# PSUM clears, column copies and delta moved out of a VectorE chain at the seam between a weight stage and the last pass

## The chip, the cores and the metric

The kernel runs on one core of one Trainium2 chip. The metric is the device time in microseconds (us), as the median of several executions. On one core there is no second die to compare, so a run counts as fast when it is within 1.5% of the fastest run of the same kernel, and only fast runs are compared.

## The reference

The reference is the forward and the backward pass of two identical layers. Each has an attention of one new token over a cached K and V, and an MLP. The output and nine gradients are wanted, among them those of both caches. All arrays are bf16.

```python
# B=2, Sq=1, D=1024; Hq=32, Hkv=4, Sk=16384, Dh=128; F=3584
def attn(x, k_cache, v_cache, wq, wo):
    q = (x @ wq) as [B, Hq, 1, Dh]
    p = softmax(q k^T * Dh**-0.5)          # each kv head serves 8 q heads
    return (p v) as [B, 1, Hq*Dh] @ wo
def mlp(x, w1, b1, w2, b2):
    return gelu(layernorm(x) @ w1 + b1) @ w2 + b2
x = x + attn(layernorm(x), ...); x = x + mlp(x, ...)     # layer 1
x = x + attn(layernorm(x), ...); x = x + mlp(x, ...)     # layer 2, same weights and caches
# outputs: x, and the vjp of (x, K, V, wq, wo, w1, b1, w2, b2) with grad_out
```

For the backward pass of attention, "do" is the gradient of o (what comes back through wo, unnormalised here, then scaled), "delta" is the sum over the head dimension of do times o, and "ds" is p times (do v - delta). The gradients of K and V need ds and p for both layers, so they are made in one last pass over the caches.

## The kernel before

The program is ordered by hand. Everything that lies in SBUF comes from pools opened once, and a pool begins where the one ahead of it ends. The seven rotating load tiles ("ld") take every chunk of the caches and of the weights that is not kept in SBUF, 1 MB or 0.9 MB each. Ahead of them lie the pools of constants and vectors. The cuts of code leave lines out ("..."), and most comments in them are added for the reader.

```python
LDW = 4096
NLD = 7
const = ctx.enter_context(tc.tile_pool(name="const", bufs=1))
vec = ctx.enter_context(tc.tile_pool(name="vec", bufs=1))
pers = ctx.enter_context(tc.tile_pool(name="pers", bufs=1))
ld = ctx.enter_context(tc.tile_pool(name="ld", bufs=NLD))       # [128, 4096] bf16: 8192 bytes a partition
res = ctx.enter_context(tc.tile_pool(name="res", bufs=1))       # kept chunks of K and V
ktp = ctx.enter_context(tc.tile_pool(name="ktp", bufs=4))
...
e_all = pers.tile([128, G, NP, 2, 8, 2], BF16, name="e_all")
hot3 = const.tile([128, 128], BF16, name="hot3")
...
        t = held_tiles[keep] if keep else ld.tile([128, LDW], BF16, name="kv_" + w, tag="ld")
```

The seam that the change is about is the end of the wo stage of layer 1 and the start of the last pass. A row of wo is either turned by TensorE and multiplied there, or dotted by VectorE:

```python
            self.dotted = range(4, self.J, 5)          # of wo's 32 rows: 4, 9, 14, 19, 24, 29
...
    for j in range(4, wob.J):
        ...
        wob.products(j, dops, gA_all[:, :, lsl(0)])    # TensorE, for rows that are not dotted
    only["e"] = None
    TP = [pt([128, 8, 128], BF16, "tpm%d" % i) for i in range(2)]
    for t in TP:
        V.memset(t[:].bitcast(F32), 0.0)               # two PSUM tiles cleared by VectorE
    do_delta(0, pairs(dops, HQ), wob)                  # dof, doT_bf, dprod, sum, split of delta
    ...
    cols = {}                                          # the columns that TensorE transposes
    for w in "VK":
        cols[w] = vec.tile([128, G, 2, 8], BF16, name="cols" + w)
        for k in range(2):
            src = saved["a%d" % k]["qT_bf" if w == "K" else "doT_bf"]
            V.tensor_copy(out=cols[w][:, :, k, :], in_=src[:])
    ...
    qs = [make_qm(w, order[0]) for w in "VK"]          # transposes of the columns
    for c in range(NCH):
        ...                                            # scores, + delta, ds
```

Copies out of PSUM are shared between ScalarE and VectorE by a running estimate of each engine's load (`load`), unless `only["e"]` names one engine.

## Time and profile before

| | before |
|---|---|
| time, median of three runs | 1166.01 us (1165.72 to 1171.62) |
| span of the profiled run | 1165.4 us |
| read from and written to HBM | 348.14 MB, 98.58 MB |
| TensorE, VectorE, ScalarE busy | 82%, 55%, 48% |

The prediction shows the rows of the page for clock and transfers, the stretches from 720 us on, and the timeline of the seam. What it does not show is how the long loading stages ahead of the seam run. These are three of their stretches before the change, in the view of busy time by stretches (columns as the prediction explains them):

```profile
20.00:100.00 80.00, 64.23 (x1335) 55.70 (x1336) 34.45 (x72) 32.25 (x128) 0.00 (x0) 0.94 1.01 419
100.00:200.00 100.00, 81.07 (x1521) 64.84 (x1520) 39.32 (x92) 38.67 (x187) 0.00 (x0) 0.77 1.02 414
300.00:400.00 100.00, 86.92 (x1720) 71.30 (x1717) 47.49 (x105) 44.82 (x199) 0.00 (x0) 0.90 1.01 418
```

The last three columns are clock, DMA share and GB/s. The DMA engines are busy all the time (1.01, 1.02) while TensorE has room (64.23 of 80 us). So the bytes that the DMA engines move per microsecond set the pace of these stages, and the number to keep in mind is 414 to 419 GB/s at a full share. The page's groups agree: TensorE's largest waits here are for load tiles (the last two columns are the idle time just before the group and what ended most of it).

```profile
L418 PE MATMUL tp<-ident,kv_V 128*128 128x128 bf16 x864 | 70.3, 227 | 10.0 <-DMA kv_V<-in_A_v_cache_dram 8.2
...
L450 PE MATMUL acc_all<-kv_V,e_all 128*16 128x256 bf16 x864 | 45.8, 292 | 28.7 <-DMA kv_V<-in_A_v_cache_dram 16.9
```

### The profile page before, as it was taken

The page shows a single profiled execution, that of the slowest core. Times are in us where ns is not written, and L with a number is a line of the kernel's source. Part 1 is how long each engine was busy: PE and PEld are TensorE (multiplying, and loading weights), DVE is VectorE, ACT ScalarE, POOL GpSimd, SP SyncE. Part 2 cuts the span into 40 slices and gives each one's busy share as a digit, 9 for nine tenths or more (in the row PEclk, how much of TensorE's full clock was granted, in tenths as well). Part 3 has the DMA queues.
Part 4 walks back from the last instruction along what each step waited for, and adds up shares of the span by engine and source line. Part 5 has one row for each costly group of instructions (what it writes and reads, how often), then busy time and mean ns, then how long its engine had stood idle before and what let it go on. Part 6 is the DMA issues. An engine that isn't in the chain of part 4 may idle for free. (4 is left out here: it accounts for less than half of the span.)

```text
span 1165.4 us, 39945 instructions
## 1 busy us (share of the span) xinstructions
PE 955.5 (82%) x17565; PEld 733.2 (63%) x17565; DVE 639.5 (55%) x1344; ACT 562.3 (48%) x1410; POOL 63.9 (5%) x113
## 2 busy tenths in 40 slices
PE   4888895497879875889987799788998988998786
PEld 3866773487767765888776688565555554555452
DVE  1545451133545433454845355867777877787674
ACT  0544351022535430344554444467677866686673
POOL 0000000000000000000000000001111111111111
PEclk9988785587988875999998889797777877797795
DMA  9999999998999989999999999687999999999996
GB/s 370 418 419 418 419 419 397 395 360 352 418 419 414 418 306 418 388 357 408 365 414 412 338 353 350 251 325 299 374 402 422 419 419 418 420 421 418 422 419 247
DMA packets 89130, 449.30 MB, mean 386 GB/s; under 512 B 7026, under 2 KB 7026, under 8 KB 49788
## 3 DMA queue, kind: packets, MB, share of 16 engines
q1 hardware_dynamic: 72204, 348.17, 74.9%
q0 software_dynamic: 16752, 98.59, 20.6%
q8 instruction: 137, 2.24, 0.8%
q14 instruction: 37, 0.30, 0.1%
HBM read 348.14 MB, written 98.58 MB: 383 GB/s over the span
## 5 line engine op out<-in xcount | busy, mean ns | idle before, releaser
L152 ACT COPY kT<-tp 128x512 int32<-128x512 int32 x209 | 122.8, 587 | 257.5 <-PE tp L418 246.5
L155 DVE COPY kT<-tp 128x1024 bf16<-128x1024 bf16 x159 | 108.6, 691 | 112.2 <-PE tp L418 99.2
L418 PE MATMUL tp<-ident,kv_K 128*128 128x128 bf16 x1728 | 147.1, 235 | 3.5 <-DMA kv_K<-in_A_k_cache_dram 3.5
L418 PEld LDWEIGHTS <-kv_K 128*128 128x128 bf16 x1728 | 111.6, 105 | 4.1 <-DMA kv_K<-in_A_k_cache_dram 4.1
L163 DVE CAST big<-xm 128x512 bf16<-128x512 f32 (+1 forms) x138 | 89.8, 685 | 31.3 <-PE xm L1222 14.4
L160 ACT CAST big<-xm 128x512 bf16<-128x512 f32 (+1 forms) x159 | 86.7, 594 | 27.8 <-PE xm L1081 16.8
L571 PEld LDWEIGHTS <-kT 128*128 128x128 bf16 x2048 | 76.7, 98 | 28.0 <-issue 22.1
L571 PE MATMUL sc<-qT_bf,kT 128*128 128x8 bf16 x2048 | 92.1, 171 | 0.7 <-issue 0.7
L268 PE MATMUL wtp<-ident,wt 128*128 128x128 bf16 x928 | 77.1, 231 | 3.7 <-issue 2.4
L418 PE MATMUL tp<-ident,kv_V 128*128 128x128 bf16 x864 | 70.3, 227 | 10.0 <-DMA kv_V<-in_A_v_cache_dram 8.2
L304 PEld LDWEIGHTS <-wt 128*128 128x128 bf16 x1696 | 49.0, 103 | 46.0 <-issue 14.7
L535 ACT ACTIVATE e_all<-sc,negm 128x64 bf16<-128x64 f32 x256 | 77.2, 345 | 1.2 <-DVE negm L530 1.2
L163 DVE CAST keepK<-xm 128x512 bf16<-128x512 f32 x94 | 61.1, 685 | 16.1 <-PE xm L1222 12.4
L450 PE MATMUL acc_all<-kv_V,e_all 128*16 128x256 bf16 x864 | 45.8, 292 | 28.7 <-DMA kv_V<-in_A_v_cache_dram 16.9
L155 DVE COPY wT<-wtp 128x1024 bf16<-128x1024 bf16 (+1 forms) x65 | 41.5, 645 | 48.7 <-PE wtp L268 45.2
L152 ACT COPY wT<-wtp 128x512 int32<-128x512 int32 (+1 forms) x59 | 33.5, 568 | 69.2 <-PE wtp L268 60.5
L160 ACT CAST keepK<-xm 128x512 bf16<-128x512 f32 x103 | 55.4, 592 | 22.4 <-PE xm L1222 21.3
L160 ACT CAST keepV<-xm 128x512 bf16<-128x512 f32 (+1 forms) x91 | 49.4, 594 | 34.9 <-PE xm L1222 28.8
L418 PEld LDWEIGHTS <-kv_V 128*128 128x128 bf16 x864 | 55.5, 102 | 11.8 <-DMA kv_V<-in_A_v_cache_dram 8.9
L163 DVE CAST keepV<-xm 128x512 bf16<-128x512 f32 (+1 forms) x81 | 52.8, 685 | 18.1 <-PE xm L1222 14.1
L268 PEld LDWEIGHTS <-wt 128*128 128x128 bf16 x928 | 58.9, 103 | 4.4 <-issue 2.9
L535 ACT ACTIVATION_READ_ACCUMULATOR e_all<-sc,negm 128x1 f32 x256 | 60.2, 235 | 0.0
(344 smaller groups left out, 1774.2 us busy)
## 6 DMA issues: line engine op xcount, KB each, us to landing
kv_K<-in_A_k_cache_dram SPq DMA_DIRECT2D x81, 1024.0 KB, 12.3
kv_V<-in_A_v_cache_dram SPq DMA_DIRECT2D x81, 1024.0 KB, 12.1
out_dram<-big POOLq DMA_DIRECT2D x36, 1024.0 KB, 17.7
wt<-in_A_wo_dram SPq DMA_DIRECT2D x32, 1024.0 KB, 10.3
wt<-in_B_w_dram SPq DMA_DIRECT2D x32, 896.0 KB, 14.3
out_dram<-keepK POOLq DMA_DIRECT2D x22, 1024.0 KB, 17.3
out_dram<-keepV POOLq DMA_DIRECT2D x18, 1024.0 KB, 16.2
wt<-in_A_wq_dram SPq DMA_DIRECT2D x16, 1024.0 KB, 9.1
```

The costliest lines, as they stand in the source:

```text
L152: S.copy(out=dst.bitcast(I32), in_=src.bitcast(I32))
L155: V.tensor_copy(out=dst, in_=src)
L160: S.copy(out=dst, in_=src)
L163: V.tensor_copy(out=dst, in_=src)
L268: PE.transpose(tp[:, o, :], wv[:, j, (o0 + o) * 128:(o0 + o + 1) * 128], ident[:])
L304: PE.matmul(fps[:, jo, :].rearrange("p (a b) -> p a b", b=2), lhsT=wv[:, j, jo * 128:(jo + 1) * 128], rhs=xT_bf[:, j0 + j, :].unsqueeze(1) ...
L418: PE.transpose(tp[:, j, :], cv[:, b * 8 + j, :], ident[:])
L450: PE.matmul(self.acc[cg:cg + 16, :], lhsT=coef(u), rhs=self.cv[:, t:t + 2, :].rearrange("p t d -> p (t d)"), start=False, stop=True, tile_ ...
L535: S.activation(out=e_all[:, g, f * half:(f + 1) * half, l, h, :], in_=sc[g][f][:, h, :].rearrange("p (a b) -> p a b", b=2), func=ACT.Exp, ...
L571: PE.matmul(sc[g][f][:, :, t % TH], lhsT=kT[:, j, :], rhs=q_bf[:, g, :], start=True, stop=True)
```

## The change

The change is meant to shorten the VectorE chain of the seam. Row 29 of wo is turned rather than dotted. The two clears go to ScalarE, as copies of a zero constant. The columns are written straight from dof, and the other column copies go ahead of an earlier stage. Delta is split after the transposes have been issued. The balance of copies is reset at each switch.

```diff
     e_all = pers.tile([128, G, NP, 2, 8, 2], BF16, name="e_all")
+    zero1 = const.tile([128, 1], F32, name="zero1")
+    V.memset(zero1[:], 0.0)
...
+    def copies_on(e):
+        only["e"] = e
+        load["A"] = load["D"] = 0.0
...
-            self.dotted = range(4, self.J, 5)
+            self.dotted = range(4, FJ, 5)              # FJ = 28: row 29 of wo is turned
...
-        doT_bf = vec.tile([128, G, 8], BF16, name=f"doT_bf{l}")
-        V.tensor_copy(out=doT_bf[:], in_=dof[:])       # (layer 1's tile goes; cols["V"] takes its place)
...
+    cols = {}                                          # now ahead of the w1 pass
...
-    only["e"] = None
+    copies_on(None)
     TP = [pt([128, 8, 128], BF16, "tpm%d" % i) for i in range(2)]
     for t in TP:
-        V.memset(t[:].bitcast(F32), 0.0)
-    do_delta(0, pairs(dops, HQ), wob)
+        S.copy(out=t[:].bitcast(F32), in_=zero1[:].to_broadcast([128, 512]))
+    dof = do_scaled(0, pairs(dops, HQ), wob,
+                    lambda b, dof: do_store(0, dof[:, b * HKV:(b + 1) * HKV], cols["V"][:, b * HKV:(b + 1) * HKV, 0, :]))
+    dl_bank = delta_mm(0, dof)
...
     qs = [make_qm(w, order[0]) for w in "VK"]
+    delta(0, dl_bank)
     for c in range(NCH):
```

More of the change, by code (lines that the diff above doesn't have):

```diff
@@ L830, in attn_out_bwd, with do_scaled @@
         _, dops = w_pass(A_wo, HD, D, "do_ps", gT_bf=gA_all[:, :, lsl(l)])
-        return do_delta(l, dops)
-    def do_delta(l, dops, ahead=None):
+        doT_bf = saved[f"a{l}"]["doT_bf"] = vec.tile([128, G, 8], BF16, name=f"doT_bf{l}")
+        dof = do_scaled(l, dops)
+        do_store(l, dof[:], doT_bf[:])
+        delta(l, delta_mm(l, dof))
+        return doT_bf
+    def do_scaled(l, dops, ahead=None, half=lambda b, dof: None):
         sv = saved[f"a{l}"]
         dof = wrk.tile([128, G, 8], F32, name="dof")
-        for b in range(2):
+        for b in (1, 0):
             V.tensor_tensor(out=dof[:, b * HKV:(b + 1) * HKV, :].rearrange("p k r -> p (k r)"), in0=dops[:, :, b],
@@ L840, in do_delta, with do_store, delta_mm, delta @@
                 r_ = sv["rbc"][:, b * HKV:(b + 1) * HKV, :].rearrange("p k r -> p (k r)")
-                V.tensor_tensor(out=dof[:, b * HKV:(b + 1) * HKV, :].rearrange("p k r -> p (k r)")[:, 4:HQ:5],
-                                in0=ahead.dp[:, :, b], in1=r_[:, 4:HQ:5], op=ALU.mult)
-        doT_bf = vec.tile([128, G, 8], BF16, name=f"doT_bf{l}")
-        V.tensor_copy(out=doT_bf[:], in_=dof[:])
+                V.tensor_tensor(out=dof[:, b * HKV:(b + 1) * HKV, :].rearrange("p k r -> p (k r)")[:, 4:FJ:5],
+                                in0=ahead.dp[:, :, b], in1=r_[:, 4:FJ:5], op=ALU.mult)
+            half(b, dof)
+        return dof
+    def do_store(l, dof, dst):
+        V.tensor_copy(out=dst, in_=dof)
+    def delta_mm(l, dof, bank=None):
+        sv = saved[f"a{l}"]
         prod = wrk.tile([128, G, 8], F32, name="dprod")
         V.tensor_tensor(out=prod[:], in0=dof[:], in1=sv["oT"][:], op=ALU.mult)
-        dlp = part_sum(prod[:].rearrange("p g r -> p (g r)"), G * 8, "dl_ps")
+        bank = pm_([128, 512], F32, "dl_ps") if bank is None else bank
+        PE.matmul(bank[:, 0:G * 8], lhsT=onesf[:], rhs=prod[:].rearrange("p g r -> p (g r)"), start=True, stop=True)
+        return bank
+    def delta(l, bank):
+        dlp = bank[:, 0:G * 8]
         rest_ = wrk.tile([128, G * 8], F32, name="dl_rest")
-        V.tensor_scalar(out=rest_[:], in0=dlp[:], scalar1=-1.0, scalar2=None, op0=ALU.mult)
+        V.tensor_scalar(out=rest_[:], in0=dlp, scalar1=-1.0, scalar2=None, op0=ALU.mult)
         part = wrk.tile([128, G * 8], BF16, name="dl_part")
@@ L861, in do_delta @@
                 V.tensor_tensor(out=rest_[:], in0=rest_[:], in1=part[:], op=ALU.subtract)
-        saved[f"a{l}"]["doT_bf"] = doT_bf
-        return doT_bf
     wq_v = A_wq.rearrange("(j p) n -> p j n", p=128)
@@ L938 @@
     mlp_slope(0)
-    only["e"] = "A"
+    copies_on("A")
     g2 = attn_in_bwd(1, g3, dn1, lambda: some(rest, 2), lambda: some(rest, 3))
@@ L955 @@
         w2b.products(j, dhps, gM_all[:, :, lsl(0)])
-    only["e"] = None
+    copies_on(None)
     mlp_hidden_bwd(0, pairs(dhps, FJ), w2b)
     x4 = mlp_out(1, fps[:, 0:DJ * WIDE].rearrange("p (j b) -> p j b", b=WIDE)[:, :, 0:2])
+    cols = {}
+    for w in "VK":
+        cols[w] = vec.tile([128, G, 2, 8], BF16, name="cols" + w)
+        for k in range(2):
+            if w + str(k) != "V0":
+                V.tensor_copy(out=cols[w][:, :, k, :], in_=saved["a%d" % k]["qT_bf" if w == "K" else "doT_bf"][:])
+    dq0 = vec.tile([128, G, 8], F32, name="dqT0")
+    dn0 = vec.tile([128, DJ, 2], F32, name="dn0")
+    V.memset(dn0[:], 0.0)
     sv = saved["m0"]
@@ L967 @@
     V.tensor_copy(out=dm[:], in_=dmps[:])
-    only["e"] = "A"
+    copies_on("A")
     dn = ln_bwd(dm[:], sv["y2"][:], sv["rstd2"][:], "dn", lambda: some(rest, 2), lambda: some(rest, 3))
@@ L991 @@
         wob.products(j, dops, gA_all[:, :, lsl(0)])
-    only["e"] = None
+    copies_on(None)
     TP = [pt([128, 8, 128], BF16, "tpm%d" % i) for i in range(2)]
     for t in TP:
-        V.memset(t[:].bitcast(F32), 0.0)
-    do_delta(0, pairs(dops, HQ), wob)
+        S.copy(out=t[:].bitcast(F32), in_=zero1[:].to_broadcast([128, 512]))
+    dof = do_scaled(0, pairs(dops, HQ), wob,
+                    lambda b, dof: do_store(0, dof[:, b * HKV:(b + 1) * HKV], cols["V"][:, b * HKV:(b + 1) * HKV, 0, :]))
+    dl_bank = delta_mm(0, dof)
     rowsA = ld.tile([128, LDW], BF16, name="rowsA", tag="ld")
@@ L1153 @@
     qms = {}
-    cols = {}
-    for w in "VK":
-        cols[w] = vec.tile([128, G, 2, 8], BF16, name="cols" + w)
-        for k in range(2):
-            src = saved["a%d" % k]["qT_bf" if w == "K" else "doT_bf"]
-            V.tensor_copy(out=cols[w][:, :, k, :], in_=src[:])
     def make_qm(w, g):
@@ L1229, in kv_pair @@
             store(dst[g, :, c * TC:(c + 1) * TC, :], stgs[w, i][:].rearrange("p (t d) -> p t d", d=128), stgs[w, i])
-    dq0 = vec.tile([128, G, 8], F32, name="dqT0")
-    dn0 = vec.tile([128, DJ, 2], F32, name="dn0")
-    V.memset(dn0[:], 0.0)
     dwq_v = out_4.rearrange("(j p) n -> p j n", p=128)
```

## The prediction

> **What bounds the kernel now.** I read the page first. It has one core, so there is no die to compare; the span is 1165.4 us.
>
> ```profile
> PEclk9988785587988875999998889797777877797795
> DMA  9999999998999989999999999687999999999996
> GB/s 370 418 419 418 419 419 397 395 360 352 418 419 414 418 306 418 388 357 408 365 414 412 338 353 350 251 325 299 374 402 422 419 419 418 420 421 418 422 419 247
> ```
>
> Each column is 29.1 us. The transfers are at 9 or more of ten in nearly every slice; the last pass (gradients of the caches and weights, stores beside loads) runs at 418 to 422 GB/s. The only hole is in slices 25 to 27, about 728 to 815 us: DMA digits 6, 8, 7 and 251 to 325 GB/s. The change touches exactly that hole, so I cut it into stages with the view of busy time by stretches (columns: length; busy us of TensorE, weight loads, VectorE, ScalarE, GpSimd with instruction counts; granted clock; DMA share; GB/s).
>
> ```profile
> 720.00:741.00 21.00, 19.81 (x441) 18.68 (x441) 16.54 (x41) 16.12 (x28) 0.00 (x0) 1.00 0.93 339
> 741.00:748.00 7.00, 1.20 (x9) 0.81 (x10) 5.66 (x29) 0.00 (x0) 0.00 (x0) 0.58 0.84 349
> 748.00:764.00 16.00, 13.91 (x250) 7.96 (x249) 8.33 (x16) 5.65 (x11) 0.58 (x1) 0.54 0.23 77
> 764.00:806.00 42.00, 35.09 (x568) 24.44 (x565) 31.12 (x52) 28.07 (x55) 4.27 (x8) 0.89 0.80 316
> 806.00:845.00 39.00, 35.34 (x457) 21.50 (x450) 30.43 (x53) 28.41 (x54) 5.53 (x10) 0.77 0.99 375
> 845.00:1120.00 275.00, 239.96 (x3159) 143.46 (x3156) 208.02 (x350) 195.43 (x376) 41.49 (x70) 0.80 1.02 418
> ```
>
> Until 741 the wo stage fills TensorE (19.81 of 21). From 741 to 748 only VectorE works: 5.66 of 7 us, against 1.20 for TensorE and none for ScalarE. From 748 to 764 compute runs again but almost nothing is transferred (77 GB/s): the tiles loaded ahead have landed, and the first new store and load need finished work. From 806 on the DMA engines are full. So 741 to 748 is a pure VectorE chain, and the time it takes is not hidden. The timeline there shows it step by step (start, duration, engine, line, operation; in brackets the idle time and what ended it):
>
> ```profile
> 740.34 0.36 PE L379 MATMUL wob_b<-gA_all,wt 128*128 128x32 bf16 x8 [0.28 <-ACT wt L152]
> ...
> 742.22 0.08 DVE L337 DVE_READ_ACCUMULATOR junk<-wt,wob_g 128x1 f32 x1
> 742.40 1.03 DVE L995 MEMSET tpm<- 128x512 f32 x2
> 743.34 0.17 DVE L837 TENSOR_TENSOR dof<-wob_b,rbc 128x32 f32<-128x32 f32 x1
> ...
> 744.17 0.22 DVE L846 TENSOR_TENSOR dprod<-dof,oT 128x64 f32<-128x64 f32 x1
> ...
> 745.17 0.23 DVE L849 TENSOR_SCALAR dl_rest<-dl_ps 128x64 f32<-128x64 f32 x1 [0.78 <-PE dl_ps L182]
> ...
> 746.98 0.28 DVE L858 SCALAR_TENSOR_TENSOR dlr<-dl_part,identf,dlr 128x64 bf16<-128x64 bf16 x1
> 747.18 0.26 DVE L1160 COPY colsV<-doT_bf 128x64 bf16<-128x64 bf16 x2
> ...
> 747.49 0.27 PE L1165 MATMUL tpm<-ident,colsV 128*16 128x128 bf16 x1 [2.36 <-DVE colsV L1160]
> ...
> 748.74 0.59 PE L1261 MATMUL xm<-dlr,hot 128*128 128x512 bf16 x1
> 749.37 0.69 DVE L1265 TENSOR_TENSOR keepV<-xm,e_all 128x512 bf16<-128x512 f32 x1 [1.18 <-PE xm L1261]
> ```
>
> TensorE's last wo product ends at 740.70. VectorE is still in its row dots until 742.30, clears two PSUM tiles, scales do (dof), stores it in bf16, multiplies by o (dprod), waits for the sum over partitions, splits delta into three bf16 parts (to 747.26), and copies columns. Only then may TensorE transpose them, score the first chunk and add delta (748.74). The first ds at 749.37 is my marker: everything after it has the same TensorE order in both kernels.
>
> [...] these operations on 6 to 64 columns take 0.17 to 0.29 us each and a dependent one starts about 0.2 us after the one before. [...] No such clear is in this trace; the nearest rows, its 512-column copies out of PSUM, average 0.59 us. [...] Here TensorE idles from 740.70 to 744.44 and the per-microsecond view has the clock at 1.00 until 742, 0.57 in the next, then 0.50 until 762. [...]
>
> **The change part by part.** I compared the two programs' orders on each engine. TensorE gains only eight transposes and eight products (16 matmuls); the order of stores and loads is the same.
>
> 1. *Row 29 is turned rather than dotted.* Two dots of 1.225 us plus 0.08 for the accumulator, spaced 1.27, leave VectorE: the ten others end at 742.30 - 2.54 = 739.76. In exchange ScalarE gets one more copy (0.59; four take 2.52, so 0.63 in a row) and TensorE 16 matmuls at that pace. The wo products then end at 740.70 + 0.66 = 741.36. VectorE is no longer last; TensorE is.
> 2. *Clears to ScalarE*, idle from 740.29 to 752.72. Two of some 0.6 us after its last copy (about 741.0) end by about 742.2, before the transposes need the tiles. So dof starts at 741.36 + 0.04 = 741.40, not 743.34: **1.94 us won**.
> 3. *Store in two halves into the columns.* One VectorE operation more, mostly hidden behind independent ones: dprod was finished 1.05 us after dof began and will need about 1.26. **0.2 lost.** dprod is finished at 742.66 (before: 744.39).
> 4. *Delta after the transposes.* TensorE now goes from the partition sum (0.78 from dprod to the next VectorE start; I take 0.6, since the clock may still be whole) straight to the two transposes, and VectorE copies the two 16-row tiles (0.33) before delta. Delta starts at about 742.66 + 0.6 + 0.3 + 0.35 = 743.9 and takes the 2.09 us of before (745.17 to 747.26): 746.0. TensorE scores the first chunk (1.03) under it and waits. The delta matmul then takes 0.59 plus 0.04, so the first ds is at **746.65, not 749.37: 2.7 us earlier**. From the start of delta to ds it was 4.20 us and is now 2.75; the difference of 1.45 is the column copies, the transposes and the scores taken from behind delta.
> 5. *Column copies and a clear of dn* (four small operations, some 0.5 us) go ahead of the w1 pass. There TensorE is the full engine (18.39 of 20 us in 700 to 720) and VectorE 10.55, so nothing is charged.
> 6. *Balance reset.* In the kernel's own count ScalarE comes out of the wo stage ahead of VectorE, so QmV and blkv went to VectorE (0.41 each). Now they go to ScalarE. Of the first four evictions ScalarE takes three rather than two, 3 x 0.52 = 1.56 against 2 x 0.6: at most 0.3 later on one buffer that is not wanted first. In the rest some copies trade engines, in both directions. I count zero, with plus or minus 1 us.
>
> Sum: -2.7. Downstream: the tiles loaded ahead landed by about 748 and the first of them is wanted at 771.5, so no transfer holds the stage back when it starts 2.7 us sooner. The first store (757.95) and load (762.39) wait for compute and move along. The full-DMA phase has the same bytes and begins sooner. So I carry the 2.7 us through whole: 1166.01 - 2.7 = **1163.3 us**.
>
> **The rivals.**
> - *Absorbed later:* if the full DMA from 806 on is paced by something fixed, the start does not matter and the time stays at 1166. For it: transfer share 0.99 and more for 300 us. Against it: DMA share is only 0.23 in 748 to 764 and 0.80 to 806, so those holes move, not fill. One chance in six.
> - *The clock stays whole:* the idle piece shrinks from 3.7 us to about 1.4. If the clock does not fall, the delta matmul, the kv products and transposes of 748 to 762, which are up to half longer at 0.50, would give another 2 to 3 us: 1160.5. Against it: 743.5 to 746 is thin work, and the clock in this stage did not return for 80% busy time. One in five.
> - *ScalarE becomes the bound* through the work moved to it. Against it: in 764 to 806 it is busy 28.07 of 42 us and VectorE 31.12, so it has the more room. For it: TensorE has only four rotating PSUM buffers in the last pass, and a traded copy that comes late to one of them holds it. That could cost 1 to 2 us: 1165.
>
> **Range and chances.** Main case 1163.3; the clock pulls to 1160.5, absorption and copies to 1166. Single runs of before spread from 1165.72 to 1166.01, with one at 1171.62. Eight times in ten between 1159.8 and 1166.3. Two per cent is 23 us, while the whole chain from 740.70 to 749.37 is 8.7 us, so faster by over 2% gets 0.01 and slower 0.005.
>
> **What would show it.** Right: no VectorE clear after the dots; dots ending near 739.8; wo products near 741.4; first dof right behind them; the scores ahead of the delta matmul; ds near 746.7; the first store near 755. Step 1 is wrong if dof starts later than 742, step 4 if dprod to ds is over 4.5 us. If ds is early but the store is not, the copies of step 6 ate it; if both are early but the end is not, absorption. A clock of 1.00 in 746 to 758 would make the gain larger.

## The result, and the profile after

The changed kernel took **1152.17 us** (median of 4 runs, 1150.28 to 1155.55) against 1165.87 of the kernel before on the same chip (4 runs, 1162.14 to 1171.62). The ratio is 0.9881, with a 95% interval of 0.9833 to 0.993. A ratio is always the mean time of one kernel's fast runs over the mean of the other's fast runs of the same rounds, so it is not quite the ratio of the medians. The gain is some 13.7 us where 2.7 had been predicted, and the time lies below the whole predicted range (1159.8 to 1166.3). By the 2% measure it counts as "same", as predicted.

The rows of the page after the change, for clock and transfers:

```profile
PEclk9988895587989885899998899788677867796685
...
GB/s 372 423 425 425 424 424 412 406 355 352 424 424 424 423 340 424 385 357 407 380 419 420 339 365 353 252 329 279 392 403 422 422 419 421 424 423 419 423 423 252
```

Against the row that the prediction shows of before, the hole in slices 25 to 27 is still there (252, 329, 279). What is new stands at the left: from the second slice on, the loading stages run at 423 to 425 where they ran at 418 to 419. That is some 700 us before the seam that the change was meant to shorten. The stretches of after say the same, at the same DMA share:

```profile
20.00:100.00 80.00, 65.04 (x1356) 56.23 (x1357) 34.49 (x72) 32.45 (x128) 0.00 (x0) 0.93 1.01 424
100.00:200.00 100.00, 77.54 (x1535) 61.71 (x1532) 39.09 (x91) 38.32 (x186) 0.00 (x0) 0.81 1.02 421
300.00:400.00 100.00, 87.30 (x1762) 71.08 (x1762) 47.92 (x108) 45.79 (x198) 0.00 (x0) 0.93 1.01 424
713.00:730.70 17.70, 16.12 (x388) 15.23 (x384) 12.35 (x21) 13.42 (x25) 0.00 (x0) 1.00 0.91 341
730.70:735.00 4.30, 1.54 (x36) 1.29 (x37) 3.50 (x19) 0.53 (x2) 0.00 (x0) 0.96 0.93 389
735.00:751.00 16.00, 13.87 (x214) 7.36 (x214) 7.37 (x12) 6.51 (x13) 0.97 (x2) 0.50 0.25 89
```

The last three lines are the seam. The thin stretch of 7 us (741 to 748 before) is now one of 4.3 us, and the clock still falls to 0.50 behind it. The timeline of the seam after the change:

```profile
727.66 0.19 PE L385 MATMUL wob_b<-gA_all,wt 128*128 128x32 bf16 x1 [0.76 <-issue]
...
729.44 1.21 PE L385 MATMUL wob_b<-gA_all,wt 128*128 128x32 bf16 x32
730.12 1.11 ACT L1023 COPY tpm<-zero 128x512 f32<-128x512 f32 x2
...
730.68 0.19 DVE L847 TENSOR_TENSOR dof<-wob_b,rbc 128x32 f32<-128x32 f32 x1 [2.89 <-PE wob_b L385]
...
731.72 0.21 DVE L862 TENSOR_TENSOR dprod<-dof,oT 128x64 f32<-128x64 f32 x1
...
732.56 0.96 PE L1277 MATMUL xm<-colsV,keepV 128*128 128x16 bf16 x32
732.61 0.34 DVE L1190 COPY r16sb<-tpm 16x128 bf16<-16x128 bf16 x2 [0.36 <-PE tpm L1188]
732.88 0.20 DVE L870 TENSOR_SCALAR dl_rest<-dl_ps 128x64 f32<-128x64 f32 x1
...
734.67 0.28 DVE L879 SCALAR_TENSOR_TENSOR dlr<-dl_part,identf,dlr 128x64 bf16<-128x64 bf16 x1
735.01 0.58 PE L1281 MATMUL xm<-dlr,hot 128*128 128x512 bf16 x1 [1.48 <-DVE dlr L879]
735.63 0.69 DVE L1285 TENSOR_TENSOR keepV<-xm,e_all 128x512 bf16<-128x512 f32 x1 [0.68 <-PE xm L1281]
```

No clear stands on VectorE after the dots, and VectorE now idles 2.89 us before dof. The scores (732.56) run under the splitting of delta. The first ds comes at 735.63 rather than 749.37.

To divide the gain I use three anchors in each trace: the first wo product of this stage, the first ds, and the end.

| | before | after | won |
|---|---|---|---|
| start to first wo product | 725.0 | 713.0 | 12.0 |
| first wo product to first ds | 24.4 | 22.6 | 1.8 |
| first ds to end | 416.0 | 416.2 | -0.2 |
| span | 1165.4 | 1151.8 | 13.6 |

Most of the gain is won before the place where the change acts. The order of instructions on each engine in the forward stages is the same in both programs, but for the clear of one new constant at the start. What differs is where the tiles lie. The change adds a constant (`zero1`, which takes 32 bytes) and drops a small tile (`doT_bf` of the first layer, 128 bytes) in the pools ahead of the load tiles. In the addresses of the compiled programs, the first load tile begins at byte 58976 of each partition before and at 58880 after, 96 bytes lower. As each tile has 8192 bytes, all seven share the remainder: 58880 is a multiple of 256, and 58976 lies 96 above one.

**Theory P (placement):** the loads run faster because their SBUF destination starts at such a boundary, and this alone is worth about 10 us. **Theory S (structure):** the parts of the change win the time, and what is seen at the left is variation between runs. A third possibility is that some other tile whose place moved matters (the kept chunks, the transposed K).

### The profile page after: what moved, and what is told of

It reads as the page before. It is cut to its first block, busy times and chain, and to the rows that moved or that the text cites. A ratio compares the mean times of both kernels' runs of the same rounds, so it can differ in the third digit from the quotient of the medians.

```text
span 1151.8 us, 39974 instructions
## 1 busy us (share of the span) xinstructions
PE 957.7 (83%) x17581; PEld 730.8 (63%) x17581; DVE 634.8 (55%) x1335; ACT 566.1 (49%) x1417; POOL 63.7 (6%) x113
## 3 DMA queue, kind: packets, MB, share of 16 engines
HBM read 348.14 MB, written 98.58 MB: 388 GB/s over the span
## 5 line engine op out<-in xcount | busy, mean ns | idle before, releaser
L424 PE MATMUL tp<-ident,kv_K 128*128 128x128 bf16 x1728 | 141.6, 230 | 5.3 <-DMA kv_K<-in_A_k_cache_dram 5.2
L424 PEld LDWEIGHTS <-kv_K 128*128 128x128 bf16 x1728 | 107.4, 102 | 6.2 <-DMA kv_K<-in_A_k_cache_dram 6.1
L166 ACT CAST big<-xm 128x512 bf16<-128x512 f32 x165 | 89.9, 593 | 27.2 <-PE xm L1111 14.7
L169 DVE CAST big<-xm 128x512 bf16<-128x512 f32 x132 | 86.2, 685 | 23.0 <-PE xm L1245 10.3
L424 PE MATMUL tp<-ident,kv_V 128*128 128x128 bf16 x864 | 70.3, 229 | 11.1 <-DMA kv_V<-in_A_v_cache_dram 9.9
L310 PEld LDWEIGHTS <-wt 128*128 128x128 bf16 x1696 | 48.8, 103 | 44.4 <-issue 14.8
```

The lines of the kernel that those rows point to most:

```text
L166: S.copy(out=dst, in_=src)
L169: V.tensor_copy(out=dst, in_=src)
L310: PE.matmul(fps[:, jo, :].rearrange("p (a b) -> p a b", b=2), lhsT=wv[:, j, jo * 128:(jo + 1) * 128], rhs=xT_bf[:, j0 + j, :].unsqueeze(1) ...
L424: PE.transpose(tp[:, j, :], cv[:, b * 8 + j, :], ident[:])
```

## The experiments

Twelve kernels ran, all correct, and their profiled runs are all in the fast state. The first two batches ran on one chip, the third on another, each with the kernel before beside it. Those of one batch share the runs of the kernel before.

### First batch: placement alone, and the change without it

The kernel before was 1166.22 us in these rounds (1161.71 to 1170.68, 35 runs).

**b_al512** is the kernel before, with one unused tile ahead of the load tiles, which so begin at 59392, a multiple of 512.

```diff
     e_all = pers.tile([128, G, NP, 2, 8, 2], BF16, name="e_all")
+    pad = pers.tile([128, 104], F32, name="pad")      # 416 bytes a partition
+    V.memset(pad[:], 0.0)
```

> The kernel before with 416 unused bytes per partition put in front of the load tiles, so that they start at 59392 (a multiple of 512) and not at 58976 (96 over one); no other instruction changes but one clear of the pad at the start. Theory A (the time won ahead of the wo stage comes from where the load tiles lie in SBUF): 20 to 100 us moves 424 GB/s as after, the first wo product starts near 713 us rather than 725, and the whole takes 1154 to 1156 us. Rival B (the chip or the moment differed): 418 to 419 GB/s and 1162 to 1166 us. Rival C (the moved instructions did it): 1162 to 1166 us as well, and a_un stays near 1152.

Measured: 1154.45 us (1152.82 to 1157.13, 5 runs), ratio 0.9905 [0.9887, 0.9922]. Its stretch from 20 to 100 us:

```profile
20.00:100.00 80.00, 65.08 (x1357) 56.26 (x1358) 34.52 (x72) 32.52 (x128) 0.00 (x0) 0.93 1.01 424
```

Not one instruction of the change is in this kernel, and it has the rate of after (424) and 0.0095 x 1166.2 = 11.1 us of gain.

**b_al64** uses a pad of 96 bytes (`[128, 24]`) instead: the load tiles begin at 59072, a multiple of 64 but 192 above a multiple of 256.

> The kernel before with 96 unused bytes ahead of the load tiles: they start at 59072, a multiple of 64 but 192 over one of 256. If a 64-byte start is all that counts, this equals b_al512 (1154 to 1156 us, 424 GB/s in 20 to 100 us); if a multiple of 256 or 512 is needed, it stays at the rate of before (418 GB/s, 1163 to 1166 us). Rivals B and C: as before.

Measured: 1165.38 us (1161.4 to 1173.32, 14 runs), ratio 1.0003 [0.9987, 1.0019].

```profile
20.00:100.00 80.00, 65.64 (x1343) 56.76 (x1343) 34.55 (x72) 32.62 (x128) 0.00 (x0) 0.91 1.01 418
```

A pad as such wins nothing, and neither does a multiple of 64. The rate stays at 418.

**a_un** is the changed kernel with a pad of 96 bytes, which takes its load tiles back to 58976, where they lie in the kernel before.

```diff
     e_all = pers.tile([128, G, NP, 2, 8, 2], BF16, name="e_all")
+    pad = pers.tile([128, 24], F32, name="pad")
+    V.memset(pad[:], 0.0)
     zero1 = const.tile([128, 1], F32, name="zero1")
```

> The changed kernel with 96 unused bytes ahead of the load tiles, which puts them back at 58976, the place of before. Theory A: the forward stages fall back to 418 GB/s, the wo stage starts near 725 us, and only the gain of the chain is left: 1163 to 1164.5 us. Rivals B and C: it stays at 1151 to 1153 us.

Measured: 1162.32 us (1159.29 to 1167.66, 22 runs), ratio 0.9974 [0.9962, 0.9987]: 3.0 us of gain, where the prediction had said 2.7 (and the expectation 1163 to 1164.5 us). In its trace, which is the slowest of the 22 runs, the first wo product is at 724.7, as before, and the first ds at 747.07:

```profile
20.00:100.00 80.00, 64.57 (x1343) 55.94 (x1343) 34.46 (x72) 32.52 (x128) 0.00 (x0) 0.94 1.01 419
```
```profile
747.07 0.69 DVE L1287 TENSOR_TENSOR keepV<-xm,e_all 128x512 bf16<-128x512 f32 x1 [0.68 <-PE xm L1283]
```

**a_again** is the changed kernel unchanged, for the same rounds.

> The changed kernel once more, for the same rounds as the others: 1150 to 1153 us by every theory but B, by which it may come out at 1160 or more on another chip.

Measured: 1150.59 us (1148.75 to 1157.34, 6 runs), ratio 0.9875 [0.985, 0.9899]. The two effects multiply to 0.9905 x 0.9974 = 0.9879, so nothing is left over. Theory S falls as the account of the large part and holds for the small one.

### Second batch: which boundary, and which tiles

The kernel before was 1166.78 us here (1160.82 to 1172.83, 35 runs). All four are the kernel before with pads.

**b_al128** has a pad of 32 bytes (`[128, 8]`): the load tiles begin at 59008, 128 above a multiple of 256.

> The kernel before with 32 unused bytes ahead of the load tiles: they start at 59008, a multiple of 128, 128 over one of 256. b_al64 (a multiple of 64 alone) won nothing. If 128 is enough: 424 GB/s in 20 to 100 us and 1154 to 1156 us. If 256 is needed: 418 GB/s and 1163 to 1166 us.

Measured: 1165.96 us (1163.33 to 1170.0, 14 runs), ratio 0.9994 [0.9976, 1.0011].

```profile
20.00:100.00 80.00, 64.87 (x1335) 56.39 (x1336) 34.51 (x72) 32.28 (x128) 0.00 (x0) 0.92 1.01 419
```

**b_al256** has a pad of 160 bytes (`[128, 40]`): they begin at 59136, a multiple of 256 and not of 512.

> The same with 160 bytes: a start at 59136, a multiple of 256 but not of 512. If a boundary of 256 is the one that counts: 424 GB/s and 1154 to 1156 us; if 512 is needed: 418 GB/s and 1163 to 1166 us.

Measured: 1155.02 us (1153.14 to 1156.29, 6 runs), ratio 0.9904 [0.9881, 0.9928].

```profile
20.00:100.00 80.00, 67.15 (x1372) 58.18 (x1373) 34.77 (x73) 32.62 (x128) 0.00 (x0) 0.91 1.01 424
```

So a start on a multiple of 256 is enough in these runs: on a multiple of 128 alone nothing is won (0.9994), and one of 512 wins no more than one of 256 (0.9905 and 0.9904). Off the boundary only three places were tried: 96, 128 and 192 bytes above it, with 419, 419 and 418 GB/s in 20 to 100 us (before, b_al128, b_al64). No fall with the distance is seen there.

**b_ld512** moves only the load tiles to a multiple of 512 and leaves all pools behind them at their old remainder (96 above a multiple of 512), by a second gap. **b_res512** is the reverse: the load tiles stay at 58976, and everything behind them moves to a multiple of 512.

```diff
     ld = ctx.enter_context(tc.tile_pool(name="ld", bufs=NLD))
+    gap = ctx.enter_context(tc.tile_pool(name="gap", bufs=1))
     res = ctx.enter_context(tc.tile_pool(name="res", bufs=1))
...
     e_all = pers.tile([128, G, NP, 2, 8, 2], BF16, name="e_all")
+    pad2 = gap.tile([128, 24], F32, name="pad2")      # b_ld512; in b_res512 [128, 104], and no pad
+    V.memset(pad2[:], 0.0)
+    pad = pers.tile([128, 104], F32, name="pad")      # b_ld512 alone
+    V.memset(pad[:], 0.0)
```

> Only the seven rotating load tiles are moved to a multiple of 512; the kept tiles, the transposed copies and all later buffers stay 96 bytes over one, by a second gap. Theory A1 (the transfers into the load tiles are what is faster): forward stages at 423 to 424 GB/s and most of the 11 us, 1155 to 1158 us. Rival A2 (the buffers that the engines use, such as the transposed copies, matter): 418 GB/s and 1163 to 1166 us.

> The complement: the load tiles stay at 58976, and the kept tiles, transposed copies and later buffers are moved to a multiple of 512. Theory A1: 418 to 419 GB/s in 20 to 100 us and 1162 to 1166 us (a little may be won in the last pass, where kept tiles are loaded and stored too). Rival A2: 1154 to 1157 us.

Measured: b_ld512 1153.8 us (1152.14 to 1155.77, 6 runs), ratio 0.9896 [0.9874, 0.9918]; b_res512 1164.08 us (22 runs, 1160.51 to 1288.55; the highest is a single slow run with a granted clock of 0.548, where the others have 0.817 to 0.834, and the ratio leaves it out), ratio 0.9985 [0.9973, 0.9997]. Their stretches, b_ld512 first:

```profile
20.00:100.00 80.00, 66.54 (x1363) 57.58 (x1364) 34.55 (x73) 32.62 (x128) 0.00 (x0) 0.92 1.01 424
```
```profile
20.00:100.00 80.00, 64.23 (x1335) 55.62 (x1336) 34.51 (x72) 32.31 (x128) 0.00 (x0) 0.94 1.01 419
```

The rotating load tiles carry the effect (b_ld512 came out 1 us faster than expected). The kept chunks, transposed K and work tiles behind them are worth 0.15% (0.03 to 0.27%).

### Third batch: parts of the change, one at a time

These are the changed kernel with one part undone. The load tiles stay at 58880 in all, so that only the part differs. The kernel before was 1165.09 us (1163.74 to 1168.76, 7 runs). I read the totals with care, as each rests on four runs, and the chain from the first wo product to the first ds for the mechanism: 21.2 us in a_again. In the first trace of the same program it was 22.6, for a standstill of TensorE that is described below. So a difference in one trace counts only where the timeline shows its cause.

**c_clearV** gives the clears back to VectorE, at the same place in the program.

```diff
-        S.copy(out=t[:].bitcast(F32), in_=zero1[:].to_broadcast([128, 512]))
+        V.memset(t[:].bitcast(F32), 0.0)
```

> The changed kernel with the two PSUM clears back on VectorE; the load tiles stay where they are. From the first wo product to the first ds it takes 21.2 us in a_again. The dots end some 2.5 us before TensorE does, and two clears of 0.485 us fit into that idle time once the last turned row has been copied out: at most 0.3 us more, 1150 to 1153 us in all. If the clears stand on the path after all: 1 us more in that stretch.

Measured: 1150.41 us (1149.09 to 1156.61, 4 runs), ratio 0.9877 [0.9845, 0.9909]; chain 21.3 us. The clears (0.48 each) now nearly fit into VectorE's idle time before the last wo product, which ends at 728.90; dof starts 0.1 us later than in a_again, counted from the first wo product.

```profile
728.01 0.48 DVE L1023 MEMSET tpm<- 128x512 f32 x1 [0.52 <-ACT wt L158]
...
728.65 0.48 DVE L1023 MEMSET tpm<- 128x512 f32 x1 [0.16 <-ACT wt L158]
729.05 0.17 DVE L847 TENSOR_TENSOR dof<-wob_b,rbc 128x32 f32<-128x32 f32 x1
```

**c_dot29** gives row 29 back to VectorE's dots.

```diff
-            self.dotted = range(4, FJ, 5)
+            self.dotted = range(4, self.J, 5)
...
-  ... [:, 4:FJ:5] ...
+  ... [:, 4:HQ:5] ...
```

> The changed kernel with row 29 dotted again. VectorE ends its dots 17.3 us after the first wo product (as before), dof follows at once as the clears are on ScalarE: 17.3 + 5.0 = 22.3 to 22.4 us to the first ds, 1.1 us more than a_again; 1151 to 1154 us. If the row is worth the whole 1.94 us that was predicted for steps 1 and 2: 23.1 us.

Measured: 1155.42 us (1154.74 to 1156.99, 4 runs), ratio 0.9912 [0.9892, 0.9931]; chain 22.4 us, 1.2 more than in a_again. Its timeline shows why: dof has no idle time ahead of it, the last dot ends where dof begins.

```profile
734.40 0.08 DVE L343 DVE_READ_ACCUMULATOR junk<-wt,wob_g 128x1 f32 x1
734.40 0.18 DVE L847 TENSOR_TENSOR dof<-wob_b,rbc 128x32 f32<-128x32 f32 x1
```

The total is above the range expected (1151 to 1154 us) and some 4 us above the changed kernel's (0.9912 against 0.9875 of a_again). The chain accounts for 1.2 of that. In the trace its first wo product is also the latest of the kernels with placed loads (717.2), and the two intervals overlap, so the rest is not settled.

**c_delta** splits delta right after its sum, ahead of the copies of the transposed columns, as before the change; the columns are still stored early.

```diff
     dl_bank = delta_mm(0, dof)
+    delta(0, dl_bank)
...
     qs = [make_qm(w, order[0]) for w in "VK"]
-    delta(0, dl_bank)
```

> The changed kernel with delta split before the transposed columns are copied out. By step 4 of the prediction the splitting (2.09 us) then stands ahead of the copies and scores: the first ds 1.0 to 1.5 us later after dof (6.0 to 6.5 us rather than 5.0), 1151 to 1154 us. Rival: the scores hide it anyway, 5.0 us.

Measured: 1151.89 us (1148.64 to 1153.23, 4 runs), ratio 0.9874 [0.9846, 0.9902]; chain 20.7 us, **shorter** than with delta moved. The expectation that it would be 1.0 to 1.5 us longer failed; the rival, that the scores hide the splitting anyway, came nearer. Its timeline:

```profile
732.05 0.22 DVE L862 TENSOR_TENSOR dprod<-dof,oT 128x64 f32<-128x64 f32 x1
...
732.80 0.22 DVE L870 TENSOR_SCALAR dl_rest<-dl_ps 128x64 f32<-128x64 f32 x1 [0.53 <-PE dl_ps L864]
...
732.90 0.97 PE L1278 MATMUL xm<-colsV,keepV 128*128 128x16 bf16 x32
...
735.13 0.27 DVE L1191 COPY r16sb<-tpm 16x128 bf16<-16x128 bf16 x2
...
735.48 0.69 DVE L1286 TENSOR_TENSOR keepV<-xm,e_all 128x512 bf16<-128x512 f32 x1
```

The scores (732.90) run under the splitting here too, because the columns are ready early. From dprod to dl_rest it takes 0.75 us, against 1.16 in the changed kernel, whose two copies (0.34) stand in between.

**c_noreset** leaves the balance of the copies as it is at each switch.

```diff
     def copies_on(e):
         only["e"] = e
-        load["A"] = load["D"] = 0.0
```

> The changed kernel without the reset of the copy balance. By step 6 of the prediction: the chain to the first ds unchanged (21.2 to 22.6 us), the whole within 1.5 us of a_again, 1149 to 1154 us. Rival: the reset is what changed the long stages: 1155 us or more.

Measured: 1150.78 us (1149.81 to 1151.93, 4 runs), ratio 0.987 [0.9851, 0.9889]; chain 21.2 us. The reset is worth nothing that these runs can see.

No version clearly beats the changed kernel: the ratios of c_clearV, c_delta and c_noreset lie within the interval of a_again.

## Why the prediction was right or wrong

**The step that failed** is the frame of the sum. The prediction says: "The change touches exactly that hole, so I cut it into stages", and its sum of -2.7 has no term for the rate of the loads. It compared the order of the instructions, found "the order of stores and loads is the same", and never asked where the tiles would lie. The missing term is the load rate. An estimate from the traces, as if all reads ran at the full rate: 348.14 MB at 419 GB/s take 830.9 us and at 424 GB/s 821.1, so 9.8 us less. Measured by itself, the placement was worth 11.1 us (b_al512; b_al256 11.2). At the first wo product, the mean of the five traces with loads off the boundary is 724.3 us and that of nine on it is 714.3.

The mechanism behind the boundary is not shown by these runs. They show the boundary alone: 424 GB/s in 20 to 100 us on it, 418 to 419 off it.

**Step 1 (row 29 turned): right.** The dots ended 14.8 us after the first wo product rather than 17.3, which is the 2.5 predicted. In a_again and three of the four kernels of the third batch the wo products end at 16.2 where they ended at 15.7, so 0.5 later, where 0.66 was predicted. In the changed kernel's first trace and in a_un they end 1.2 to 1.5 later still, as TensorE stands still there, for 0.76 us once and for less at other places, without a wait that the profile shows. What causes that is open; it was not predicted, and it comes and goes between two runs of the same program. The prediction called the step wrong if dof started later than 742, and in a_un dof starts at 742.1, for this reason.

**Step 2 (clears): right in the time of dof, wrong in what earns it.** dof starts right behind the last wo product. But c_clearV shows that the clears cost only 0.1 us of chain on VectorE once row 29 is gone. The two parts cover each other. dof starts 18.4 us after the first wo product before the change, 17.2 with the clears moved alone (c_dot29), 16.3 with the row turned alone (c_clearV) and 16.2 with both (a_again). So the row alone brings the whole 2 us, and the clears alone would bring 1.1. The size of the clears was about right (1.11 us for two on ScalarE, 0.59 each, "Two of some 0.6" in the prediction), and VectorE needs even less, 0.48 each. That ScalarE can clear these PSUM tiles was not shown by the trace of before; the changed kernel, which came out correct, shows it.

**Step 3 (store in halves): right.** dprod starts 1.04 us after dof (0.83 before), the 0.2 of the prediction. (The 0.2 us from one start to the next is for dependent operations. Before the change, dprod at 744.17, which does not need the store at 744.06, began 0.11 us after it, while the store takes 0.20.)

**Step 4 (delta): right in size, wrong in reason.** From dof to the first ds it was 6.0 us, was predicted at 746.65 - 741.40 = 5.25, and measured 4.9 to 5.1. The reason was to be delta's later place. c_delta has the old place and takes 4.5, so the later place costs 0.5 us, the two copies in front of delta. The gain comes from what c_delta still has. That is the early columns above all, though no run undoes them alone, and, as it seems, some 0.2 us of a clock that is still whole when the sum over partitions runs: from dprod to dl_rest it took 1.00 us before and 0.75 in c_delta, where the two matmuls of the sum took 0.43 rather than 0.69, but 0.79 also in b_al128, the old program in a trace where the clock was still whole when that sum began (its weight loads took at most 0.19 us each, against 0.29 and 0.34 before).

**Step 5 (column copies):** no cost is seen, but no run tests it by itself. **Step 6 (reset): right**, zero within the noise.

**The sum for the structure** is then confirmed: 3.0 us measured in a_un, with the first ds at 747.07 and the first store at 755.62 (746.65 and 755 predicted). That the first ds comes so close is partly luck, as TensorE's standstill is in this trace; without it the chain takes 21.2 us, against 24.4 before and 21.7 predicted.

**The rivals.** Absorption fell: both gains reach the end. The stretch from ds to end is 412.5 to 418.8 us in all traces, on average 416.2 with the loads off the boundary and 414.5 on it. ScalarE as the bound was not seen. The whole clock fell too: it is 0.50 from 735 to 751, although the idle piece shrank as foreseen, to 1.34 and 1.48 us. Matmuls do take longer at 0.50, as that rival counts: before the change the QmV products took 0.39 us (median) in 748 to 762.4 and 0.27 in 764 to 772, where the clock is 1.00. But it took TensorE's 3.7 us of idle time as what halves the clock. That was my assumption alone, and the views do not bear it out. The stretches of one microsecond in which the clock falls, before and after:

```profile
742.00:743.00 1.00, 0.00 (x0) 0.00 (x0) 0.84 (x4) 0.00 (x0) 0.00 (x0) 0.57 0.96 401
734.00:735.00 1.00, 0.00 (x0) 0.00 (x0) 0.89 (x4) 0.00 (x0) 0.00 (x0) 0.83 0.73 303
```

A mean of 0.57 puts the fall at about 742.15, only 1.4 us after the last wo product; 0.83 puts it at about 734.66, 1.1 us after TensorE's last work (733.53). So it fell after far less than 3.7 us without work, and a shorter idle piece did not save it. It is back at 1.00 from about 762.6 before the change and 751.7 after it. What makes it fall and return is not shown by these runs.

None of the three was the way in which it went, and the probabilities of the 2% classes came out right only because the placement is worth 1% and not 2.

## What to carry to other kernels

Where loads set the pace as here, look at the address at which the load tiles begin and try it on a multiple of 256 bytes. Here rows of 8192 bytes that start on one load at 424 GB/s (20 to 100 us) and others at 418 to 419, and the whole kernel before gains about 1% (ratios 0.9905, 0.9904 and 0.9896 on it; 1.0003 and 0.9994 off it). A 32-byte constant more or a vector less moved it, and an unused tile of 160 bytes was worth more than three times what the planned change was (11.2 us against 3.0). Before crediting a change with a gain, compare the traces ahead of the place where it acts; if they differ there, pad the changed kernel back to the old addresses, and time the pad alone. When two parts remove the same wait, undo them one at a time: only one of them may be earning.
